# Decay attention with a gated expert layer: scores in four rounds of two banks, the first decay rows without TensorE, and a new order

## The chip, the cores and the metric

The kernel runs on one core of one Trainium2 chip. The metric is the device time of one execution in microseconds. Engines are named as the profile names them: PE (TensorE matmul), PEld (its weight loads), DVE (VectorE), ACT (ScalarE), POOL (GpSimd), SP (SyncE, which here only issues transfers).

## What is computed

For 8 batches of 8 heads (sequence 576, head dimension 64) the reference does this, and then an expert layer on the 128 tokens of each batch that score highest:

```python
scores = scale * q @ k.T                       # 576 x 576 for each head
cum    = cumsum(log(clip(f, 1e-4, 1)))         # 576 numbers for each head
scores = where(causal, -1e9, scores + cum[i] - cum[j])
attn   = softmax(scores); x = attn @ v         # all heads side by side: 576 x 512
s      = x @ w_gate; idx = top 128 of s
out[idx] = x[idx] + sigmoid(s[idx]) * (relu(x[idx] @ w1) @ w2)
```

The term `cum[i]` is the same for a whole row and falls out of the softmax, so the kernel only needs `-8 * cum[j]`, one row of 576 numbers for each head, spread over all 128 partitions. It calls that tile `e`.

## The kernel before, in words

The work goes in 32 pairs of heads. For a pair, `q` and `k` lie in SBUF with one head on partitions 0 to 63 and the other on 64 to 127 (tiles `rq` and `rk`). The scores of the two heads are computed together, head by head in the two halves of the array, into two PSUM banks, one for each head. There are eight banks in all. The lower triangle of a head is cut into row blocks `i` of 128 queries (`i` = 0, 1, 2, 3, and `NF` = 4 for the last 64) and these into six units, listed in `units` (L542): block 3 with keys 0 to 384, block 3 with keys 384 to 576, block 1, block 2, the 64 by 64 corner, and block 0. Each unit takes two fresh banks (two `ps` tokens).

What follows a unit:

- L631, DVE: one instruction for each head adds the decay, takes the row's extreme and writes the sum to SBUF (`p`). Its decay comes from `e`, or from `m`, which POOL makes out of `e` by masking it along the diagonal (L412). When the last such instruction on a bank is done, the bank is free.
- L684, ACT: exp over the row block, with the row sum.
- L703, PE: transposes of the exps into a pair of banks; L350 (ACT, POOL) or L354 (DVE) copies them to SBUF (`pt`).
- L786, PE: the product with `v`; copies (`ot`); L844, PE: transposes back; L849, DVE: division by the row sums.
- L859 and L863: the gate's scores; after four pairs a batch is complete and its expert layer follows (L1006 ranks, L1059 gathers, L1122 to L1183 are the matmuls, L1194 scatters).

The decay: `f` for all 64 heads is loaded with one head on each partition (L370), clipped (L373), its logarithm is taken (L380, ACT), then a running sum (L384, DVE), then times -8 (L389). The result is stored to DRAM (`eq`, L407), and for heads 2 to 63 a transfer spreads a row of `eq` over 128 partitions (L513, `e<-eq`). For heads 0 and 1 PE spreads it: `bcast` (L462) multiplies a selecting column of the identity with the rows (L470) into two banks for each head, and copies bring them to `es[0]` and `es[1]`.

The order of all this is not written out by hand. Each piece is entered with `add` (L64): its cost by engine, what it comes after, which tokens (banks, buffers) it takes and gives back, and a number `place`. `Flow.run` (L122) then lays out the schedule when the kernel is built: for each engine it looks at the pieces that could start within `EPS` of the earliest one and takes the one with the smallest `place`. An engine's instructions run in the order that comes out of this. A piece that may run on several engines goes to the one where it would end first, after `BD` microseconds have been added for DVE. Before `HALF` microseconds PE's costs count double. Some 35 constants (L212 to L256) enter the places.

Of the kernel before, what the change touches and what calls it, by code (L numbers as in the profile page):

```python
# [17 lines left out]
P = 128  # L18
# [12 lines left out]
class Flow:  # L31
# [146 lines left out]
def kernel(  # L178
# [30 lines left out]
    NRT = (cap + P - 1) // P  # L209
    FR = 3 * R  # L210

    BD = 0.595  # L212
    WP = 17
    WQ = 0
    R0 = -28.266
    X0 = -83.254
    XE_ = -237.817
    XH_ = 1.479
    XM_ = 144.372
    XB_ = -3.268  # L220
    XN_ = -284.728
    XO_ = -358.772
    XU_ = 1.204
    XQ_ = 299.353
    XR_ = 137.373
    XG_ = -107.42
    PL4 = -284.738
    GW = 587.406
    EPS = 0.121
    LOOK = 13  # L230
    PR = -110.796
    PL = 37.918
    PS = 148.049
    PV = 3.402
    PM = -218.946
    PE_ = 78.604
    PC = 15.176
    PB = -122.458
    PD = 13.682
    VO = 29.244  # L240
    VD = 1
    GD = 0.1
    WS = -43.026
    WD = 316.377
    WL = 239.211
    RK = 41.91
    RD = 9.792
    XP = 21.468
    GO = 4.807
    GS = 2.051  # L250
    GL = 29.298
    LG = 2.69
    SB = 3
    SX = 2.5
    SP = -3.444
    TU = 0.061  # L256

    const = ctx.enter_context(tc.tile_pool(name="const", bufs=1))
# [9 lines left out]
    def bank(tk):  # L268
        return banks[:, tk.at * 512:(tk.at + 1) * 512]
# [92 lines left out]
    def load(fn, kb, n=1, slow=0.0, **kw):  # L362
        return add({"sp": 0.63 * n}, fn, lat=1.6 + slow, dma=kb / 240, **kw)
# [3 lines left out]

    def t_fs(e):
        z["fs"] = moe.tile([BH, S], F32, tag="h", name="fs")
        nc.sync.dma_start(out=z["fs"], in_=f)  # L370

    def t_clamp(e):
        nc.vector.tensor_scalar(z["fs"], z["fs"], 1e-4, 1.0, ALU.max, ALU.min)  # L373

    def t_ones(e):
        z["ones"] = work.tile([BH, S], F32, tag="ot", name="ones", bufs=2)
        nc.vector.memset(z["ones"], 1.0)

    def t_ln(e):
# [1 line left out]

    def t_scan(e):
        z["cum"] = moe.tile([BH, S], F32, tag="srow", name="cum")
        nc.vector.tensor_tensor_scan(out=z["cum"], data0=z["ones"], data1=z["fs"], initial=0.0,  # L384
                                     op0=ALU.mult, op1=ALU.add)
# [5 lines left out]
    tk_h, tk_ot, tk_srow = Token("h"), Token("ot"), Token("srow")  # L391
    tk_ep = Token("hth", 3)
    d_fs = load(t_fs, 144, place=-60, take=[tk_h])
    d_ones = add({"dve": 0.6}, t_ones, place=-60, take=[tk_ot])
    d = add({"dve": 0.47}, t_clamp, after=[d_fs], place=-59)
    d = add({"act": 0.68}, t_ln, after=[d], place=-58, give=[tk_h])

    def t_warm(e):

        warm = small.tile([P, 1], F32, tag="none", name="warm", bufs=2)  # L400
        nc.scalar.activation(warm[0:BH], z["ones"][:, 0:1], AF.Exp)

    add({"act": 1.5}, t_warm, after=[d, d_ones], place=-57.5)
    d_scan = add({"dve": 1.35}, t_scan, after=[d, d_ones], place=-57, take=[tk_srow], give=[tk_ot])
    d_ep = add({"dve": 0.45}, t_ec, after=[d_scan], place=-56, take=[tk_ep], give=[tk_srow])
# [51 lines left out]

    d_zero = add({"dve": 0.4}, t_zero, place=-70)

    spread = {}  # L460

    def bcast(h):  # L462

        tk = [Token("ps") for _ in range(2)]
        st = {}

        def eb(e):
            st["b"] = [bank(t) for t in tk]
            for g in range(2):
                nc.tensor.matmul(st["b"][g][:, 0:S // 2], ident[0:BH, h:h + 1].broadcast_to([BH, P]),  # L470
                                 z["ec"][:, g * (S // 2):(g + 1) * (S // 2)], start=True, stop=True)

        def ec(e, g):
            copy_on(e, es[h][:, g * (S // 2):(g + 1) * (S // 2)], st["b"][g][:, 0:S // 2])

        x = spread[h] = add({"pe": 1.0}, eb, after=[d_ep, d_ident], place=-20 + h, take=tk, give=[tk_ep], kind="av")
        return [add({**act(S // 2), **dve(S // 2)}, lambda e, g=g: ec(e, g), after=[x], place=-50 + h, give=[tk[g]])
                for g in range(2)]

    raws, ops, tks = {}, {}, {}  # L480
    dec = {}
    decused = {}
# [1 line left out]
    def pair_ops(p):  # L484
        pl = 9 * p - PL
        r = p % 2
        tk = tks[p] = {"q": Token("rq", 6), "k": Token("raw", 6)}

        def t_k(e):
            t = raws["k", p] = rawp.tile([P, S], F32, tag="raw", name=f"rk{p}")  # L490
# [61 lines left out]
    def pair_parts(p):  # L552
# [19 lines left out]
        copied = []  # L572
        sums = []
        exps, late, scored, ready, tk_nm = {}, {}, {}, {}, {}
        for u, (i, k0, k1) in enumerate(units):
            n = k1 - k0
            t = p * NT + (AT[u] - LOOK) // 2
            ahead = [moved[min(t, len(moved) - 1)]] if t >= 0 and moved else []
            if p == 0 and u > 1:
                ahead = ahead + list(spread.values())  # L580
            place = p * NU + AT[u] * XU_ - LOOK * NU / 8
            tk_n, tk_b = [], [Token("ps"), Token("ps")]
            if i == 2 or i == 3 and k0 == 0:
                late[i] = Token(f"p{i % 2}", i)
                tk_n.append(late[i])
            if i == NF:
                late[NF] = Token("p4")
                tk_n.append(late[NF])

            def s0(e, u=u, i=i, k0=k0, tk_b=tk_b):  # L590
                st["sc", u] = [bank(t) for t in tk_b]
                if i == 2 or i == 3 and k0 == 0:
                    st["pw", i] = pw.tile([P, PAT[i] + 2 * WB[i]], F32, tag=f"p{i % 2}", name=f"p{p}_{u}", bufs=2)

            def sc(e, u=u, i=i, k0=k0, k1=k1):
                for hh in range(2):
                    rows = slice(hh * D, hh * D + D)
                    nc.tensor.matmul(st["sc", u][hh][:, 0:k1 - k0], q_rows(raws["q", p], hh, i), raws["k", p][rows, k0:k1],  # L598
                                     start=True, stop=True)

            def part(hh, i):

# [14 lines left out]

                return t if hh == 0 or i == NF else t.rearrange("p (b c) -> p b c", c=R)

            def m(e, hh, x0, x1, in1, key, first, u=u, i=i, k0=k0, into=into, blocks=blocks):  # L620
# [15 lines left out]
            if i < 2 or i == 3 and k0:  # L636
                ahead = ahead + [scored[i + 2 if i < 2 else i]]
            x2 = add(row(n), lambda e, s0=s0, sc=sc: (s0(e), sc(e)), after=ops[p] + ahead, place=place,
                     take=tk_b + tk_n, give=list(tks[p].values()), kind="row")
            scored[i] = x2  # L640
            for hh in range(2):
                h = 2 * p + hh
                def e_(n_, h=h):
# [628 lines left out]
```

## Time and profile before

| | |
|---|---|
| median of 3 runs | 419.74 us (418.47 to 420.68) |
| the profiled execution | 424.2 us, span 422.4 us |
| busy: PE / DVE / ACT / POOL | 392.2 / 324.0 / 324.3 / 210.9 us |
| weight loads on PE (PEld) | 268.8 us |

The span runs from the first to the last instruction of the execution; 1.8 us of the execution's time lie outside it. The end of a matmul is modelled, so the busy time of PE tells less than the waits of its weight loads.

### The profile page before, as it was taken

The page shows a single profiled execution, that of the slowest core. Times are in us where ns is not written, and L with a number is a line of the kernel's source. Part 1 is how long each engine was busy: PE and PEld are TensorE (multiplying, and loading weights), DVE is VectorE, ACT ScalarE, POOL GpSimd, SP SyncE. Part 2 cuts the span into 40 slices and gives each one's busy share as a digit, 9 for nine tenths or more (in the row PEclk, how much of TensorE's full clock was granted, in tenths as well). Part 3 has the DMA queues.
Part 4 walks back from the last instruction along what each step waited for, and adds up shares of the span by engine and source line. Part 5 has one row for each costly group of instructions (what it writes and reads, how often), then busy time and mean ns, then how long its engine had stood idle before and what let it go on. Part 6 is the DMA issues. An engine that isn't in the chain of part 4 may idle for free. (4 is left out here: it accounts for less than half of the span.)

```text
span 422.4 us, 12058 instructions
## 1 busy us (share of the span) xinstructions
PE 392.2 (93%) x3873; PEld 268.8 (64%) x3873; DVE 324.0 (77%) x1356; ACT 324.3 (77%) x1008; POOL 210.9 (50%) x368
## 2 busy tenths in 40 slices
PE   4689999899999899899999999999999999999995
PEld 3266765566656675566576676757666675768773
DVE  3577668787998699889968977789776987688721
ACT  4699999999999787999697888879797887712220
POOL 5486786977686642655156355423646323223100
PEclk9889999999999999999999999999999999999998
DMA  6688778888687636775375636655565403202100
GB/s 199 187 223 236 193 215 234 240 225 242 195 238 201 196 113 189 212 194 165 113 203 172 190 104 177 198 171 137 172 167 189 119 30 111 90 25 82 50 25 26
DMA packets 76870, 68.10 MB, mean 161 GB/s; under 512 B 47715, under 2 KB 56966, under 8 KB 76806
## 3 DMA queue, kind: packets, MB, share of 16 engines
q1 hardware_dynamic: 75446, 62.98, 52.5%
q0 software_dynamic: 1280, 4.20, 2.9%
q8 instruction: 31, 0.51, 0.5%
q14 instruction: 33, 0.27, 0.2%
q10 hardware_dynamic: 80, 0.15, 0.1%
HBM read 55.59 MB, written 11.70 MB: 159 GB/s over the span
## 5 line engine op out<-in xcount | busy, mean ns | idle before, releaser
L684 ACT ACTIVATE p<-p,nm 128x576 f32<-128x576 f32 (+4 forms) x288 | 165.4, 581 | 13.1 <-DVE nm L631 12.9
L412 POOL TENSOR_SCALAR_AFFINE_SELECT m<-e 128x384 f32<-128x384 f32 (+3 forms) x256 | 108.3, 449 | 112.7 <-DMA e<-eq 73.8
L598 PE MATMUL banks<-rk,rq 64*128 64x192 f32 (+4 forms) x768 | 127.5, 429 | 13.0 <-DMA rq<-in_qk_dram 5.3
L350 ACT COPY pt<-banks 128x512 f32<-128x512 f32 (+4 forms) x311 | 113.0, 428 | 16.7 <-PE banks L703 12.1
L631 DVE CUSTOM_DVE_ANT_0 p<-banks,m 64x64 f32<-64x64 f32 (+3 forms) x256 | 99.8, 419 | 14.5 <-PE banks L598 6.9
L598 PEld LDWEIGHTS banks<-rk,rq 64*128 64x128 f32 x768 | 71.8, 190 | 45.7 <-DVE nm L631 16.0
L786 PE MATMUL banks<-pt,v 128*64 128x448 f32 (+4 forms) x768 | 92.3, 392 | 0.6 <-DVE nm L631 0.5
L786 PEld LDWEIGHTS banks<-pt,v 128*64 128x64 f32 x768 | 47.2, 137 | 44.7 <-issue 27.1
L703 PE MATMUL banks<-ident,p 64*128 64x64 f32 x1472 | 68.4, 229 | 6.7 <-DVE nm L631 4.1
L703 PEld LDWEIGHTS banks<-ident,p 64*128 64x128 f32 x1472 | 59.7, 140 | 19.6 <-DVE nm L631 8.6
L859 POOL TENSOR_TENSOR gj<-x,wg 128x640 f32<-128x640 f32 x32 | 49.4, 1545 | 43.5 <-DVE x L849 26.5
L684 ACT ACTIVATION_READ_ACCUMULATOR p<-p,nm 128x1 f32 x288 | 55.8, 194 | 0.0
L631 DVE CUSTOM_DVE_ANT_0 p<-banks,e 128x384 f32<-128x384 f32 x64 | 35.2, 552 | 13.2 <-ACT e L350 4.0
L1006 DVE TENSOR_SCALAR_CACHE_REDUCE j<-srow,sg 128x384 uint8<-128x384 f32 (+6 forms) x72 | 41.2, 572 | 2.0
L849 DVE TENSOR_TENSOR x<-banks,rn 128x640 f32<-128x640 f32 x32 | 26.3, 822 | 17.7 <-PE banks L844 11.1
L350 ACT COPY ot<-banks 128x128 f32<-128x128 f32 (+1 forms) x58 | 20.3, 394 | 14.5 <-PE banks L786 14.4
L631 DVE DVE_READ_ACCUMULATOR2_ANT nm<- 128x1 f32 (+1 forms) x384 | 31.2, 81 | 0.0
L631 DVE CUSTOM_DVE_ANT_0 p<-banks,m,nm 128x192 f32<-128x192 f32 x64 | 26.6, 416 | 5.5 <-DVE nm L631 1.0
L863 DVE TENSOR_REDUCE gu<-gj 128x5 f32<-128x640 f32 x32 | 25.8, 805 | 5.0 <-POOL gj L859 4.6
L1194 POOL DMA_INDIRECT out_dram<-xe,idx x8 | 8.2, 1022 | 38.3 <-DVE xe L1190 34.9
L1122 PE MATMUL banks<-w1h,xth 128*128 128x512 f32 x64 | 26.0, 406 | 0.9 <-ACT xth L1084 0.7
L1175 PE MATMUL banks<-w2h,hth 128*128 128x512 f32 x64 | 26.2, 409 | 0.0
(91 smaller groups left out, 416.1 us busy)
## 6 DMA issues: line engine op xcount, KB each, us to landing
e<-eq SPq DMA_DIRECT2D x62, 288.0 KB
rk<-in_qk_dram SPq DMA_DIRECT2D x32, 288.0 KB
out_dram<-x SPq DMA_DIRECT2D x16, 512.0 KB
rq<-in_qk_dram SPq DMA_DIRECT2D x32, 144.0 KB
rq<-in_qk_dram SPq DMA_DIRECT2D x32, 128.0 KB
v<-in_v_dram SPq DMA_DIRECT2D x32, 128.0 KB
v<-in_v_dram SPq DMA_DIRECT2D x32, 80.0 KB
srow<-sd SPq DMA_DIRECT2D x7, 320.0 KB
```

Source lines behind the costliest of these rows:

```text
L350: nc.scalar.copy(d, s_)
L412: nc.gpsimd.affine_select(out=dst, in_=src, pattern=w, compare_op=ALU.is_ge, fill=NEG, base=base, channel_multiplier=1)
L598: nc.tensor.matmul(st["sc", u][hh][:, 0:k1 - k0], q_rows(raws["q", p], hh, i), raws["k", p][rows, k0:k1], start=True, stop=True)
L631: nc.vector.tensor_tensor_reduce(out=into(hh, i, r_, x0, x1), in0=blocks(b_[r_, x0 - k0:x1 - k0], hh, i), in1=blocks(in1(), hh, i), scale= ...
L684: nc.scalar.activation(x, x, AF.Exp, bias=st["nm", hh, i], scale=-1.0, accum_out=l)
L703: nc.tensor.transpose(tp[:, g, col:col + R], src, ident[g * R:g * R + R, g * R:g * R + R])
L786: nc.tensor.matmul(avb[p, g][par * D:(par + 1) * D, qo + q0 - g * SPL:qo + q1 - g * SPL], vt[:, j, par * D:(par + 1) * D], pt[:, off:off + ...
L849: nc.vector.tensor_tensor(out=xhs[key][:, :, w_ * P:(w_ + 1) * P].rearrange("p c (h d) -> p c h d", h=2), in0=st["tb"][:, :, 0:NCH * D].re ...
L859: nc.gpsimd.tensor_tensor(out=gj, in0=xhs[key][:, :, w0:w1], in1=wg[:, hb * HB + w0:hb * HB + w1].unsqueeze(1).broadcast_to([P, NCH, P]), ...
L1006: nc.vector.tensor_scalar(junk[0:n, 0:w, :], src, sg()[0:n, c:c + 1], None, op, ALU.add, accum_out=cnt[0:n, k, c:c + 1])
L1122: nc.tensor.matmul(q["hp", n][0:nr, :], q["xth"][:, c, 0:nr], r_[:, c, cs], start=(c == 0 and k_ == 0), stop=False)
L1175: nc.tensor.matmul(q["yp"][0:nr, :], q["hth"][:, c, 0:nr], r_[:, c, :], start=(c == 0 and k_ == 0), stop=False)
```

## The change

1. The six units become four groups. Two groups consist of two units each, which share a round's two banks side by side: block 3's keys 384 to 576 (192 columns) with block 1 (320 columns), and block 0 (192) with the corner (64).
2. For heads 0 and 1 the row of `f` is spread over 128 partitions by a transfer, and clip, logarithm, running sum and factor are computed on all partitions (DVE, ACT, DVE, ACT), straight into `es[0]` and `es[1]`. `bcast` and its matmuls, banks and copies go. The computation for all 64 heads stays, since `eq` feeds the others; its load of `f` is issued by ACT's queue.
3. `HALF`, `EPS`, `BD` and nearly all constants of the places get other values, so that the order of every engine is laid out anew.

```diff
-    HALF = 22.0
+    HALF = 12.0
...
-    BD = 0.595
+    BD = 14.28
...
-    EPS = 0.121
+    EPS = 0.003
...
     def t_fs(e):
         z["fs"] = moe.tile([BH, S], F32, tag="h", name="fs")
-        nc.sync.dma_start(out=z["fs"], in_=f)
+        nc.scalar.dma_start(out=z["fs"], in_=f)
...
+    def first(h):
+        e_, m_ = es[h], ms[h][:, 0:S]
+        def f_clamp(e):
+            (nc.vector if e == "dve" else nc.gpsimd).tensor_scalar(e_, e_, 1e-4, 1.0, ALU.max, ALU.min)
+        def f_ln(e):
+            nc.scalar.activation(e_, e_, AF.Ln)
+        def f_scan(e):
+            nc.vector.tensor_tensor_scan(out=m_, data0=z["ones"], data1=e_, initial=0.0, op0=ALU.mult, op1=ALU.add)
+        def f_ec(e):
+            nc.scalar.mul(e_, m_, -8.0)
+        x = load(lambda e: nc.sync.dma_start(out=e_, in_=f[h:h + 1, :].broadcast_to([P, S])), 288, place=-62 + h)
+        x = add({"dve": 0.6}, f_clamp, after=[x], place=-59.5 + h)
+        x = d_lf[h] = add({"act": 0.53}, f_ln, after=[x], place=-59 + h)
+        x = add({"dve": 1.35}, f_scan, after=[x, d_ones], place=-58.5 + h, give=[tk_ot])
+        return add({"act": 0.53}, f_ec, after=[x], place=-58 + h)
+    d_first = [first(h) for h in range(2)]
...
-    add({"act": 1.5}, t_warm, after=[d, d_ones], place=-57.5)
+    add({"act": 1.5}, t_warm, after=[d, d_ones] + list(d_lf.values()), place=-58.6)
...
-    def bcast(h):
...
-                le = bcast(h)
+                le = [d_first[hh]]
...
-    units = [(3, 0, 384), (3, 384, S), (1, 0, 320), (2, 0, 448), (NF, 0, R), (0, 0, FR)]
-    AT = (0, 1, 2, 4, 5, 6)
+    groups = [[(3, 0, 384)], [(3, 384, S), (1, 0, 320)], [(2, 0, 448)], [(0, 0, FR), (NF, 0, R)]]
+    AT = (0, 1, 4, 5)
...
+            tk_n, tk_b = [], [Token("ps", len(group)), Token("ps", len(group))]
...
+            def sc(e, u=u, group=group, tk_b=tk_b):
+                st["sc", u] = [bank(t) for t in tk_b]
+                o = 0
+                for i, k0, k1 in group:
...
+                    for hh in range(2):
+                        rows = slice(hh * D, hh * D + D)
+                        nc.tensor.matmul(st["sc", u][hh][:, o:o + k1 - k0], q_rows(raws["q", p], hh, i), raws["k", p][rows, k0:k1],
+                                         start=True, stop=True)
+                    o += k1 - k0
```

## Rows read from the trace of the kernel before

**Rows 1.** The page's busy times: us, share of the span, instructions

```profile
span 422.4 us, 12058 instructions
PE 392.2 (93%) x3873; PEld 268.8 (64%) x3873; DVE 324.0 (77%) x1356; ACT 324.3 (77%) x1008; POOL 210.9 (50%) x368
```

**Rows 2.** Windows: stretch, its us, then busy us (instructions) PE, PEld, DVE, ACT, POOL

```profile
25.00:50.00 25.00, 24.54 (x280) 17.15 (x280) 18.94 (x87) 24.45 (x80) 19.43 (x31) 0.96 0.77 214
50.00:75.00 25.00, 24.18 (x288) 15.83 (x286) 18.45 (x77) 23.85 (x80) 16.59 (x27) 1.00 0.79 224
75.00:100.00 25.00, 23.48 (x305) 15.81 (x303) 18.93 (x82) 23.62 (x79) 19.58 (x33) 1.00 0.83 225
...
200.00:250.00 50.00, 49.12 (x498) 33.70 (x499) 42.83 (x193) 40.34 (x124) 19.69 (x34) 1.00 0.52 149
```

**Rows 3.** Timeline of the start: start us, us, engine, line; idle before it, releaser

```profile
0.74 0.60 SPq L370 DMA_DIRECT2D fs<-in_f_dram  x1
3.62 0.45 DVE L373 TENSOR_SCALAR fs<-fs 64x576 f32<-64x576 f32 x1 [1.79 <-DMA fs<-in_f_dram]
4.11 0.68 ACT L380 ACTIVATE fs<-fs 64x576 f32<-64x576 f32 x1 [2.09 <-DVE fs L373]
4.81 1.28 ACT L401 ACT_TABLE_LOAD   x1
4.82 1.35 DVE L384 TENSOR_TENSOR_SCAN cum<-ones,fs 64x576 f32<-64x576 f32 x1 [0.75 <-ACT fs L380]
...
6.21 0.62 DVE L389 TENSOR_SCALAR ec<-cum 64x576 f32<-64x576 f32 x1
...
9.95 0.56 DVE L631 CUSTOM_DVE_ANT_0 p<-banks,e 128x384 f32<-128x384 f32 x1 [3.13 <-ACT e L350]
...
12.10 0.61 SPq L513 DMA_DIRECT2D e<-eq  x1
...
12.34 0.56 DVE L631 CUSTOM_DVE_ANT_0 p<-banks,e 128x384 f32<-128x384 f32 x1 [0.85 <-ACT e L350]
...
20.80 0.56 DVE L631 CUSTOM_DVE_ANT_0 p<-banks,e 128x384 f32<-128x384 f32 x1 [3.04 <-DMA e<-eq]
```

**Rows 4.** Waits of PE's weight loads, 25 to 350 us: total us, times, longest

```profile
PEld banks L598 <- DVE nm L631: 11.0, 27, 0.8
PEld banks L598 <- ACT pt L350: 10.2, 28, 0.8
```

**Rows 5.** The same waits, 140 to 350 us

```profile
PEld banks L598 <- ACT pt L350: 6.4, 17, 0.8
PEld banks L598 <- DVE nm L631: 4.7, 14, 0.6
PEld banks L598 <- DVE x L849: 3.3, 6, 1.0
```

**Rows 6.** DVE's copies (L354) by stretch: us, busy us (count)

```profile
25.00:50.00 25.00, 1.31 (x2) 0.96 0.77 214
50.00:75.00 25.00, 1.36 (x3) 1.00 0.79 224
75.00:100.00 25.00, 1.57 (x3) 1.00 0.83 225
```

**Rows 7.** ACT's lines 25 to 125 us, the copy that most resembles them: busy, mean ns

```profile
L350 ACT COPY pt<-banks 128x512 f32<-128x512 f32 x20 | 10.9, 589 | 0.6 <-DVE pt L354 0.6
```

**Rows 8.** Lines of DVE in the first 25 us: a reduction of 192 columns and its read-out

```profile
L631 DVE CUSTOM_DVE_ANT_0 p<-banks,m,nm 128x192 f32<-128x192 f32 x4 | 1.7, 416 | 0.4 <-PE banks L470 0.2 <-DVE nm L631 0.2
L631 DVE DVE_READ_ACCUMULATOR2_ANT nm<- 128x1 f32 x18 | 1.5, 81 | 0.0
```

**Rows 9.** Timeline at 209 us: turns in one pair of banks, and the copies of its halves

```profile
209.13 0.66 PE L703 MATMUL banks<-ident,p 64*128 64x64 f32 x16
...
209.84 1.07 ACT L350 COPY pt<-banks 128x512 f32<-128x512 f32 x2 [0.39 <-PE banks L703]
```

**Rows 10.** PE's lines over the whole span: the matmuls of the 320-column unit

```profile
L598 PE MATMUL banks<-rk,rq 64*128 64x320 f32 x128 | 29.7, 483 | 3.5 <-DVE x L849 1.4 <-ACT pt L350 1.3 <-DVE nm L631 0.3
```

More of the change, by code (lines that the diff above doesn't have):

```diff
@@ L210 @@
     FR = 3 * R
-    BD = 0.595
+    BD = 14.28
     WP = 17
     WQ = 0
[L215 to L228, printed above, removed]
-    EPS = 0.121
-    LOOK = 13
[L231 to L240, printed above, removed]
+    R0 = -77.756
+    X0 = -68.439
+    XE_ = -327.929
+    XH_ = 7.854
+    XM_ = 53.367
+    XB_ = -7.168
+    XN_ = -63.025
+    XO_ = -208.515
+    XU_ = 1.335
+    XQ_ = 493.393
+    XR_ = 125.313
+    XG_ = 21.837
+    PL4 = -478.193
+    GW = 98.553
+    EPS = 0.003
+    LOOK = 13
+    PR = -210.485
+    PL = -23.333
+    PS = 534.017
+    PV = 76.813
+    PM = -72.798
+    PE_ = 32.812
+    PC = -113.684
+    PB = -32.5
+    PD = -24.608
+    VO = 5.153
     VD = 1
     GD = 0.1
[L243 to L251, printed above, removed]
+    WS = -47.45
+    WD = 405.121
+    WL = 461.576
+    RK = 62.425
+    RD = 6.657
+    XP = 4.552
+    GO = 25.288
+    GS = 0.584
+    GL = 84.612
     LG = 2.69
@@ L254 @@
     SX = 2.5
-    SP = -3.444
+    SP = -185.065
     TU = 0.061
@@ L389, in t_ec @@
         nc.vector.tensor_scalar(z["ec"], z["cum"], -8.0, None, ALU.mult)
[L391 to L393 removed]
+    tk_h, tk_ot, tk_srow = Token("h"), Token("ot", 3), Token("srow")
+    tk_ep = Token("hth")
+    def first(h):
[13 more added lines that the diff above has]
+        return add({"act": 0.53}, f_ec, after=[x], place=-58 + h)
@@ L394 @@
+    d_lf = {}
+    d_fs = add({"act": 0.62}, t_fs, place=-63, take=[tk_h], lat=2.2)
     d_ones = add({"dve": 0.6}, t_ones, place=-60, take=[tk_ot])
-    d = add({"dve": 0.47}, t_clamp, after=[d_fs], place=-59)
-    d = add({"act": 0.68}, t_ln, after=[d], place=-58, give=[tk_h])
+    d_first = [first(h) for h in range(2)]
+    d = add({"dve": 0.47}, t_clamp, after=[d_fs], place=-60.6)
+    d = add({"act": 0.68}, t_ln, after=[d], place=-60.5, give=[tk_h])
     def t_warm(e):
         warm = small.tile([P, 1], F32, tag="none", name="warm", bufs=2)
-        nc.scalar.activation(warm[0:BH], z["ones"][:, 0:1], AF.Exp)
@@ L403 @@
-    add({"act": 1.5}, t_warm, after=[d, d_ones], place=-57.5)
-    d_scan = add({"dve": 1.35}, t_scan, after=[d, d_ones], place=-57, take=[tk_srow], give=[tk_ot])
-    d_ep = add({"dve": 0.45}, t_ec, after=[d_scan], place=-56, take=[tk_ep], give=[tk_srow])
+        nc.scalar.activation(warm[0:BH], z["ones"][0:BH, 0:1], AF.Exp)
+    add({"act": 1.5}, t_warm, after=[d, d_ones] + list(d_lf.values()), place=-58.6)
+    d_scan = add({"dve": 1.35}, t_scan, after=[d, d_ones], place=-58.2, take=[tk_srow], give=[tk_ot])
@@ L407 @@
+    d_ep = add({"dve": 0.45}, t_ec, after=[d_scan], place=-58.1, take=[tk_ep], give=[tk_srow])
     st_eq = add({"act": 0.62}, lambda e: nc.scalar.dma_start(out=eq[:, :], in_=z["ec"]), lat=2.5, after=[d_ep], place=PR,
@@ L458 @@
     d_zero = add({"dve": 0.4}, t_zero, place=-70)
-    spread = {}
-    def bcast(h):
[L464 to L478, printed above, removed]
     raws, ops, tks = {}, {}, {}
@@ L574, in pair_parts @@
         exps, late, scored, ready, tk_nm = {}, {}, {}, {}, {}
-        for u, (i, k0, k1) in enumerate(units):
-            n = k1 - k0
+        plan = []
+        for u, group in enumerate(groups):
             t = p * NT + (AT[u] - LOOK) // 2
             ahead = [moved[min(t, len(moved) - 1)]] if t >= 0 and moved else []
-            if p == 0 and u > 1:
-                ahead = ahead + list(spread.values())
             place = p * NU + AT[u] * XU_ - LOOK * NU / 8
[L582 to L590, printed above, removed]
-                st["sc", u] = [bank(t) for t in tk_b]
[L592 to L599, printed above, removed]
@@ new lines, in pair_parts @@
+            tk_n, tk_b = [], [Token("ps", len(group)), Token("ps", len(group))]
+            for i, k0, _ in group:
+                if i == 2 or i == 3 and k0 == 0:
+                    late[i] = Token(f"p{i % 2}", i)
+                    tk_n.append(late[i])
+                elif i == NF:
+                    late[NF] = Token("p4")
+                    tk_n.append(late[NF])
+                elif i < 2 or i == 3:
+                    ahead = ahead + [scored[i + 2 if i < 2 else i]]
+            def sc(e, u=u, group=group, tk_b=tk_b):
+                st["sc", u] = [bank(t) for t in tk_b]
+                o = 0
+                for i, k0, k1 in group:
+                    if i == 2 or i == 3 and k0 == 0:
+                        st["pw", i] = pw.tile([P, PAT[i] + 2 * WB[i]], F32, tag=f"p{i % 2}", name=f"p{p}_{u}", bufs=2)
+                    for hh in range(2):
[3 more added lines that the diff above has]
+                    o += k1 - k0
@@ L601, in part @@
+            x2 = add({"pe": sum(row(k1 - k0)["pe"] for _, k0, k1 in group)}, sc, after=ops[p] + ahead, place=place,
+                     take=tk_b + tk_n, give=list(tks[p].values()), kind="row")
+            o = 0
+            for i, k0, k1 in group:
+                scored.setdefault(i, x2)
+                plan.append((u, i, k0, k1, o, x2, tk_b, place))
+                o += k1 - k0
+        for u, i, k0, k1, co, x2, tk_b, place in plan:
             def part(hh, i):
@@ L618, in blocks, with m @@
                 return t if hh == 0 or i == NF else t.rearrange("p (b c) -> p b c", c=R)
-            def m(e, hh, x0, x1, in1, key, first, u=u, i=i, k0=k0, into=into, blocks=blocks):
+            def m(e, hh, x0, x1, in1, key, first, u=u, i=i, k0=k0 - co, into=into, blocks=blocks):
                 b_ = st["sc", u][hh]
@@ L634, in m @@
                 st["nm", hh, i] = nm if i < NF else t[:, g:g + 1]
[L636 to L640, printed above, removed]
             for hh in range(2):
```

6 lines of the change are left out of this document (3 added, 3 removed).

## Prediction

> **What bounds the kernel now.** I read the page's busy times first [rows 1]. PE is busy 93% of the span, but its weight loads only 64%; so PE is seldom without a matmul in flight, and yet its queue often stands at a load. The windows by stage [rows 2] come next, since the share of the span is a mean. Two stages differ. From 25 to 100 us ACT is busy 24.45 + 23.85 + 23.62 = 71.92 of 75 us, 96%, while DVE stays at 75%: ACT sets the pace, and only 3.1 us of it are free. In the stretch at 200 to 250 us ACT has fallen to 40.34 of 50 and DVE to 42.83, and PE shows 49.12: the expert layers now run between the pairs, and what PE waits for decides. The waits of the weight loads say what that is: a new round of scores needs two free banks and finds them still held by a DVE reduction (L631), an ACT copy (L350) or DVE's division (L849) [rows 4, 5]. The start [rows 3] is a stage of its own: DVE's first reduction begins at 9.95, after 3.13 us in which it waited for the decay of head 0, then it waits 0.85 us for head 1 and, in pair 1, 3.04 us for a transfer from `eq`. After the attention only expert layers are left; the change touches nothing there but their places.
>
> The Trainium skill (Perfetto Trace Analysis, Identifying the Most-Contended Engine) says that matmul busy time is a bad measure of PE's distance from its limit and names the weight loads' busy share instead. By that, 93% would leave nothing to gain and 64% does leave something; the waits below show the same without it.
>
> **The change, part by part.**
>
> *The start.* Before, the chain to `e` of head 0 is load, clip 0.45, logarithm 0.68, sum 1.35, factor 0.62, then PE and copies, to 9.95 [rows 3]. After, PE and the copies fall out, but DVE computes three times instead of once: 3 x 0.45 + 3 x 1.35 + 0.62 = 6.0 us where 2.4 stood (the durations on 64 partitions are taken for 128, as both have 576 columns). Its input lands no sooner than 3.62, so all three are through at 9.6 at the earliest. ACT has three logarithms (2.04), then the table load 1.28 that the exp needs, then the factor, for which I take the logarithm's 0.68: from 4.11, one clip after landing, that is 4.11 + 2.04 + 1.28 + 0.68 = 8.1, and some 0.6 more if the spread load, twice as large as the 144 KB one, lands later. So `e` of head 0 can be there at 8.1 to 8.7 and that of head 1 some 0.7 us later, where the second reduction on an `e` began at 12.34. But the three scans stand ahead of the reductions on DVE unless the third is put behind, and then `eq` is late. Bounds: 1.3 us before 9.95 and the 0.85 us gap may go, and the 3.04 us wait in pair 1 if its load is issued sooner; what is gained ahead of that wait is lost in it unless it goes too, so the gain is at most 3.0 us. At the other end `ec` ends at 9.6 instead of 6.8, 2.8 us later; the first `e<-eq` was issued at 12.10, and with a store that lands as long after its issue as the load of `f` did (2.9 us), it can't go before 12.6 to 13.1: 1.0 us lost. I take 1.0 gained, the middle. The two spread loads put 1.2 us (two issues of 0.60) ahead of `rk` and `rq` on SP's queue; PE's scores then come that much later and still stand ready before DVE is. That cover is gone only if the reductions begin before about 8 us. The load of `f` moves from SP to ACT's queue, ahead of the table load there, and costs 0.6 us that the transfer's landing hides.
>
> *Four rounds for six.* Matmuls, reductions and exps are the same in number and size, so no engine's work shrinks. What can go is the wait for banks: 192 rounds become 128. In 25 to 350 us the loads of L598 waited 11.0 + 10.2 = 21.2 us for reductions and copies [rows 4]; a third of it is 7.1 us, the upper bound. In the first stage ACT sets the pace and a PE that waits less waits elsewhere, so I count from 140 us on: 6.4 + 4.7 + 3.3 = 14.4 [rows 5], a third is 4.8 us. The lower bound is nothing, since each remaining round holds its banks over two reductions. I take 4.8: a second unit in the same banks asks for no free bank at all.
>
> *Copies.* With `BD` at 14.28 a copy goes to DVE only where ACT is that far behind, which is never; `BD` was 0.595. In 25 to 100 us DVE made 2 + 3 + 3 = 8 copies [rows 6]. On ACT the nearest row is 0.589 us each [rows 7]: 4.7 us more on an engine with 3.1 us free. Later ACT has room. The ends are 0 (the copies fall where ACT would wait for a transpose) and 4.7; I take 2.4, the middle, as no row shows the exchange.
>
> *Places.* The new constants reorder everything. They add no instruction, and no row prices them; their bounds are those of the rivals.
>
> Sum: 424.2 (the profiled execution, span 422.4 and 1.8 around it) - 1.0 - 4.8 + 2.4 = 420.8. The median of the runs is 4.5 below the profiled execution, so 416.3, 0.8% less than 419.74. What this kernel's measurement can tell from no change is about 0.5%, 2.1 us: faster means under 417.6, slower over 421.8.
>
> **The rivals.**
>
> *All of it is collected.* The start gives 3.0, the rounds 7.1, the copies fall into waits: -10.1, so 409.6. For it: the waits are spread over 55 places of at most 0.8 us [rows 4], such as an order laid out anew can cover. Against it: ACT at 96% in the first stage.
>
> *ACT keeps the pace.* The rounds give nothing, since what PE saves it waits at the next transpose for ACT; -1.0 + 2.4 = +1.4, so 421.1. For it rows 2, first stage; against it the fall of ACT to 81% later.
>
> *The reader waits for the whole bank.* In a shared round DVE's reduction of the first 192 columns may have to wait until PE has written the second part. At 209 us [rows 9] both halves of a pair of banks were copied only after the last of 16 turns (209.13 + 0.66, copy at 209.84), though the first half was written by half of them. The second part's matmul is 0.483 us [rows 10], in 32 rounds; if as many of them are exposed as rounds waited before (55 of 192, 0.29), that is 32 x 0.29 x 0.483 = 4.5 us. It eats the rounds' gain: -1.0 - 4.8 + 2.4 + 4.5 = +1.1, so 420.8.
> The Trainium skill (PSUM — Partial Sum Buffer, PSUM bank collisions raise a hardware error) asks for guards by bank and quadrant, not by address, which would make every such reduction wait so; the copies in rows 9 agree with it.
>
> *Held banks: slower.* Place: the 64 two-part rounds. Each bank is held for one more reduction, 0.416 + 0.081 = 0.50 us [rows 8], and the round behind it, which needs two, comes later by that wherever it waited already: 64 x 0.29 = 18.6 rounds, 9.3 us. -1.0 - 4.8 + 2.4 + 9.3 = +5.9, so 425.6. For it: L631 is the first among those waited for [rows 4]. Against it: a round that is written later also takes its banks for fewer separate turns. It decides from 0.29 us for each of these rounds on: 18.6 x 0.29 = 5.3, which undoes the 3.4 us gained and adds the 2.1 that can be told.
>
> **How the numbers follow.** Forecast 0.40 (its own range 413 to 419); all collected 0.20; ACT keeps the pace 0.13; whole bank 0.10; held banks 0.17. Faster: 0.32 of the forecast's 0.40 and 0.20, together 0.52, with 0.01 from the others. Same: 0.08 of the forecast, 0.16 of the two cases near 421. Slower: 0.17 and the rest of those two, 0.23. The range reaches from 407, a little under the case with all collected (the places have no price), to 425, near the held banks' 425.6; outside are about 0.08 below and 0.10 above.
>
> **What would show it.** No L470; the first reduction on an `e` near 9 us, with three scans ahead of it, and the next no longer behind a gap; ACT 96% or more busy from 25 to 100 us and no L354 copies; waits of L598's loads for L631, L350 and L849 from 140 us on down from 14.4 to about 10 us; the last product with `v` some 3 us sooner. Wrong it would be if L598's waits stay or grow (held banks), if L631 waits more for L598 (whole bank), if the first 100 us get longer (copies), or if the time comes from the last expert layers, for which I count nothing.

## The result, and the profile after

The changed kernel takes 425.43 us (median of 4 runs, 424.19 to 426.11) against 420.21 us for the kernel before beside it (4 runs): ratio 1.0128, 95% interval [1.0088, 1.0168]. On two other chips it came to 1.0070 [1.0038, 1.0101] and 1.0082 [1.0041, 1.0123]. It is about 0.9% slower, some 4 us; 0.8% faster was forecast, and 425.43 lies just outside the range. Executions that took over 1.5% more than the fastest of their kernel are left out of the ratios (of the twelve of k2 below six, of h1's three), and the ratios are not quite the quotients of the medians. The two profiled executions are not a measure of the change: that of before stood 4.5 us above its median, that of the changed kernel (425.63 us, span 423.9) on it.

The page's busy times, in the columns of [rows 1]:

```profile
span 423.9 us, 11994 instructions
PE 387.1 (91%) x3865; PEld 276.8 (65%) x3865; DVE 311.3 (73%) x1343; ACT 328.6 (78%) x1024; POOL 211.4 (50%) x369
```

DVE has 12.7 us less and PE 5.1 us less to do than before, ACT 4.3 us more, and the span is longer. So PE and DVE, with less to do, wait more. The windows, in the columns of [rows 2] (the value behind the engines is the granted clock):

```profile
25.00:50.00 25.00, 22.57 (x248) 15.44 (x248) 16.12 (x75) 23.93 (x77) 13.77 (x22) 0.93 0.79 232
50.00:75.00 25.00, 22.33 (x262) 14.71 (x262) 18.65 (x89) 24.89 (x83) 21.98 (x32) 1.00 0.81 230
75.00:100.00 25.00, 22.55 (x255) 15.49 (x251) 16.43 (x74) 22.15 (x74) 16.43 (x30) 0.93 0.76 212
```

ACT is busy 23.93 + 24.89 + 22.15 = 70.97 of 75 us from 25 to 100, about what it was (71.92). In the same stretch PE issued 248 + 262 + 255 = 765 matmuls where [rows 2] have 873. The start, in the columns of [rows 3]:

```profile
0.73 0.56 ACTq L370 DMA_DIRECT2D fs<-in_f_dram  x1
...
0.74 0.88 SPq L410 DMA_DIRECT2D e<-in_f_dram  x2
...
5.90 0.45 DVE L373 TENSOR_SCALAR fs<-fs 64x576 f32<-64x576 f32 x1 [4.06 <-DMA fs<-in_f_dram]
...
7.10 1.35 DVE L384 TENSOR_TENSOR_SCAN cum<-ones,fs 64x576 f32<-64x576 f32 x1 [0.38 <-ACT fs L380]
8.37 1.33 DVE L405 TENSOR_TENSOR_SCAN m<-ones,e 128x576 f32<-128x576 f32 x1
...
8.74 4.65 PE L604 MATMUL banks<-rk,rq 64*128 64x384 f32 x16 [8.74 <-DMA rq<-in_qk_dram]
...
11.02 1.60 DVE L405 TENSOR_TENSOR_SCAN m<-ones,e 128x576 f32<-128x576 f32 x1 [0.60 <-ACT e L402]
...
12.54 0.53 DVE L648 CUSTOM_DVE_ANT_0 p<-banks,e 128x384 f32<-128x384 f32 x1
...
14.28 1.58 SPq L518 DMA_DIRECT2D e<-eq  x3
```

The three sums stand ahead of the first reduction (L648 is the old L631), which starts at 12.54 where [rows 3] have 9.95. Of these 2.6 us, 2.3 come from the first clip (5.90 for 3.62): it waited 4.06 us for `f`. From the clip on, the chain takes 12.54 - 5.90 = 6.64 us, before 9.95 - 3.62 = 6.33: three sums on DVE cost what the detour over PE and the copies cost. The issue of `e<-eq` moved from 12.10 to 14.28. The views of the two loads say how long they took:

```profile
L370 ACTq DMA_DIRECT2D fs<-in_f_dram x1: 565/565/565, 0.7 to 0.7; - x1
...
DMA to landing us min/median/max: 5.1/5.1/5.1
...
L410 SPq DMA_DIRECT2D e<-in_f_dram x2: 402/412/421, 0.7 to 1.2; - x2
...
DMA to landing us min/median/max: 5.4/5.4/5.4
```

The load of `f` landed 2.9 us after its issue (0.74 to 3.62) when it was the first on SP's queue and the next load was issued 0.65 us later. It takes 5.1 us from ACT's queue, beside the two spread loads of 288 KB. The waits of the weight loads ahead of score rounds (L604 is the old L598), 140 to 350 us, in the columns of [rows 5]:

```profile
PEld banks L604 <- DVE nm L648: 3.2, 9, 0.7
PEld banks L604 <- ACT pt L350: 1.8, 5, 0.5
PEld banks L604 <- DVE x L861: 1.3, 2, 1.0
```

These are 6.3 us where [rows 5] sum to 14.4: 8.1 us gone, more than the 4.8 of the forecast. What came in their place is on DVE. First the kernel before, then the changed one: DVE's reductions by form, 25 to 380 us; the columns are busy time, mean ns of one, and the idle time before them with its releasers.

```profile
L631 DVE CUSTOM_DVE_ANT_0 p<-banks,m 128x448 f32<-128x448 f32 x60 | 35.9, 617 | 1.6 <-PE banks L598 0.9 <-PE banks L703 0.5 <-ACT p L684 0.3
L631 DVE CUSTOM_DVE_ANT_0 p<-banks,e 128x384 f32<-128x384 f32 x60 | 32.9, 551 | 5.8 <-PE banks L598 3.5 <-DMA rq<-in_qk_dram 1.6 <-issue 0.4
...
L631 DVE CUSTOM_DVE_ANT_0 p<-banks,m,nm 128x192 f32<-128x192 f32 x60 | 24.9, 416 | 5.1 <-PE banks L598 1.0 <-DVE nm L631 0.9 <-ACT pt L350 0.3
...
DVE p L631 <- PE banks L598: 11.2, 27, 1.7
```

```profile
L648 DVE CUSTOM_DVE_ANT_0 p<-banks,m 128x448 f32<-128x448 f32 x61 | 37.6, 618 | 13.5 <-PE banks L604 13.2 <-issue 0.3
L648 DVE CUSTOM_DVE_ANT_0 p<-banks,e 128x384 f32<-128x384 f32 x60 | 32.5, 553 | 14.7 <-PE banks L604 10.9 <-ACT pt L350 3.0 <-ACT s L350 0.3
...
L648 DVE CUSTOM_DVE_ANT_0 p<-banks,m,nm 128x192 f32<-128x192 f32 x60 | 24.8, 414 | 6.8 <-PE banks L604 3.1 <-POOL m L437 1.6 <-POOL gj L871 1.2
...
DVE p L648 <- PE banks L604: 30.3, 24, 5.2
```

The last line of each is from the list of DVE's waits in the same stretch: total us, times, longest. DVE waited 11.2 us for scores and now waits 30.3, in fewer and longer waits. PE waits less for banks, and DVE waits more for PE. Whether it is the rounds, the start or the order that does this, this profile can't tell, since all three changed at once.

### The profile page after: what moved, and what is told of

Read it like the earlier page. It is cut to its first block, busy times and chain, and to the rows that moved or that the text cites. A ratio compares the mean times of both kernels' runs of the same rounds, so it can differ in the third digit from the quotient of the medians.

```text
span 423.9 us, 11994 instructions
## 1 busy us (share of the span) xinstructions
PE 387.1 (91%) x3865; PEld 276.8 (65%) x3865; DVE 311.3 (73%) x1343; ACT 328.6 (78%) x1024; POOL 211.4 (50%) x369
## 5 line engine op out<-in xcount | busy, mean ns | idle before, releaser
L696 ACT ACTIVATE p<-p,nm 128x320 f32<-128x320 f32 (+4 forms) x288 | 166.8, 586 | 6.7 <-DVE nm L648 6.1
L604 PE MATMUL banks<-rk,rq 64*128 64x192 f32 (+4 forms) x768 | 123.2, 433 | 16.4 <-DMA rq<-in_qk_dram 8.7
L350 ACT COPY pt<-banks 128x256 f32<-128x256 f32 (+4 forms) x320 | 120.3, 430 | 14.5 <-PE banks L715 12.9
L648 DVE CUSTOM_DVE_ANT_0 p<-banks,m 128x320 f32<-128x320 f32 (+3 forms) x256 | 99.0, 418 | 20.9 <-PE banks L604 17.3
L604 PEld LDWEIGHTS banks<-rk,rq 64*128 64x128 f32 x768 | 79.1, 198 | 37.1 <-DVE nm L648 13.3
L715 PEld LDWEIGHTS banks<-ident,p 64*128 64x128 f32 x1472 | 63.2, 143 | 22.6 <-issue 6.9
L715 PE MATMUL banks<-ident,p 64*128 64x64 f32 x1472 | 71.5, 231 | 7.0 <-ACT pt L350 2.6
L798 PEld LDWEIGHTS banks<-pt,v 128*64 128x64 f32 x768 | 45.9, 137 | 47.8 <-issue 30.7
L648 DVE CUSTOM_DVE_ANT_0 p<-banks,e 128x384 f32<-128x384 f32 x64 | 34.7, 553 | 16.4 <-PE banks L604 12.7
L350 ACT COPY ot<-banks 128x128 f32<-128x128 f32 x64 | 23.1, 402 | 21.1 <-PE banks L798 21.0
L861 DVE TENSOR_TENSOR x<-banks,rn 128x640 f32<-128x640 f32 x32 | 26.2, 822 | 13.6 <-PE banks L856 11.5
L648 DVE CUSTOM_DVE_ANT_0 p<-banks,m,nm 128x192 f32<-128x192 f32 x64 | 26.5, 414 | 8.6 <-PE banks L604 4.3
L648 DVE DVE_READ_ACCUMULATOR2_ANT nm<- 128x1 f32 (+1 forms) x384 | 31.0, 81 | 0.0
L1147 ACT ACTIVATE h<-banks 128x512 f32<-128x512 f32 x16 | 9.6, 602 | 20.9 <-PE banks L1141 20.9
```

Source lines behind the costliest of these rows:

```text
L604: nc.tensor.matmul(st["sc", u][hh][:, o:o + k1 - k0], q_rows(raws["q", p], hh, i), raws["k", p][rows, k0:k1], start=True, stop=True)
L648: nc.vector.tensor_tensor_reduce(out=into(hh, i, r_, x0, x1), in0=blocks(b_[r_, x0 - k0:x1 - k0], hh, i), in1=blocks(in1(), hh, i), scale= ...
L696: nc.scalar.activation(x, x, AF.Exp, bias=st["nm", hh, i], scale=-1.0, accum_out=l)
L715: nc.tensor.transpose(tp[:, g, col:col + R], src, ident[g * R:g * R + R, g * R:g * R + R])
L798: nc.tensor.matmul(avb[p, g][par * D:(par + 1) * D, qo + q0 - g * SPL:qo + q1 - g * SPL], vt[:, j, par * D:(par + 1) * D], pt[:, off:off + ...
L861: nc.vector.tensor_tensor(out=xhs[key][:, :, w_ * P:(w_ + 1) * P].rearrange("p c (h d) -> p c h d", h=2), in0=st["tb"][:, :, 0:NCH * D].re ...
```

## The experiments

Theory S (start): the loss comes from the landing of `f` and all that hangs on it. Theory O (order): it comes from the order laid out anew. Rival R (rounds): the shared banks cost more than they bring. Rival D: DVE's sums standing in a row cost the time, not the landing. The expectations call the order theory P (for places) in the first runs (f1 to f6), and the landing theory L in h1 and h2. Ratios are to the kernel before on the same chip, with 95% intervals.

### One part alone, the order laid out anew each time

Four kernels keep two of the three parts or one, and the planner lays out a new order for each:

```diff
 f1:  after, with
-    groups = [[(3, 0, 384)], [(3, 384, S), (1, 0, 320)], [(2, 0, 448)], [(0, 0, FR), (NF, 0, R)]]
+    groups = [[(3, 0, 384)], [(3, 384, S)], [(1, 0, 320)], [(2, 0, 448)], [(NF, 0, R)], [(0, 0, FR)]]
 f2:  after, with
-                le = [d_first[hh]]
+                le = bcast(h)                     # and the load of f on SP's queue again
 f3:  after, with the constants of before
 f4:  before, with first(h) in place of bcast(h); its constants stay
```

> The changed kernel with six rounds of scores again; new start and new places stay. Theory P (the new places cost the time): still slow, 424 to 427 us, and DVE still waits some 30 us for score matmuls, since the order by places and not the rounds makes the scores late. Theory R (rounds shared by two units hold banks longer and make the reader wait for the whole bank): the 5.2 us come back, 419 to 422 us, and the reductions of 192 columns wait for PE as little as before (1.0 us in all, 4.3 after the change). Theory S (the start costs it): 424 to 426 us, the first reduction still at 12.5 us.

> The changed kernel with the decay of heads 0 and 1 spread by PE again; four rounds and new places stay. Theory S: the first reduction comes back from 12.5 to about 10 us and the time falls by about that, 2.5 us, to some 423 us. Theories P and R: what the start loses is given back in the first 150 us, where ACT sets the pace; 425 us, within 1 us of the changed kernel.

> The changed kernel's four rounds and new start, with all constants of the places (and HALF, EPS, BD) as before. Theory P: back to 419 to 422 us or under it, and DVE's wait for score matmuls back towards 11 us. Theory R: 424 us or more, since the shared rounds are still there. Theory S: 422 to 423 us.

> The kernel before with nothing changed but the start (heads 0 and 1 computed on all partitions, three loads of f). Theory S: 2 to 3 us slower than before, 422 to 423 us, with the first reduction near 12.5 us. Theories P and R: no difference from before that can be told, 419 to 421 us.

Measured: six rounds (f1) 1.0256 [1.0226, 1.0287]; old start (f2) 1.0110 [1.0070, 1.0150]; old constants (f3) 1.0206 [1.0160, 1.0252]; only the start (f4) 1.0190 [1.0143, 1.0237]. Then the other two single parts, and the kernel before once more, for a second trace:

```diff
 f5:  before, with the four rounds; its constants stay, and
-            if p == 0 and u > 1:
+            if p == 0 and u > 0:
 f6:  before, with the constants of after
```

> The kernel before with nothing changed but the rounds: four of two banks instead of six. Since the planner found no way with its old condition, the second round of pair 0, too, comes after the spreading of heads 0 and 1 by PE. Theory R: slower than before, 424 us or more, the reductions of 192 columns waiting for PE. Theory P: no slower than before, 416 to 421 us, and fewer waits of weight loads for banks.

> The kernel before, six rounds and old start, with the new constants alone. Theory P: 424 us or more, DVE waiting 20 to 30 us for score matmuls. Theory R or S: 419 to 422 us.

> The kernel before once more with a profile, as a second trace beside the first, whose own time of 424.2 us lies 4 us above the median. If that trace is usual: 422 us of span again and the same waits. If it is not: a span of 417 to 419 us, and the difference shows in which stage the first trace lost time that other executions do not lose.

Measured: only the rounds (f5) 1.0105 [1.0084, 1.0125]; only the constants (f6) 1.0254 [1.0229, 1.0278]; before again (f7) 422.28 us beside a median of 422.54. Every cell is slower than the kernel before; four of the six are slower than all parts together (1.0128 at most), and f2 and f5 are about as slow. Read as prices the three single parts would add to 5.5%, where all three at once cost 1%. So these cells don't price the parts: each has an order of its own that no one fitted to it. How much that can be, the smallest edit shows.

### The same pieces in a slightly other order

```diff
-    EPS = 0.121
+    EPS = 0.15
```

> The kernel before with EPS 0.15 instead of 0.121 and nothing else: the same pieces, the same start and rounds, only laid out in another order from the early pairs on. Theory O (an order is fitted to its constants, and any other costs): 1.010 to 1.025, as in the runs in which one part was changed under constants fitted to another. If an order laid out anew costs nothing by itself: 0.996 to 1.004.

Measured: 1.0416 [1.0373, 1.0460]. No piece's work is changed, only which ready piece is taken first and, for a few copies, the engine (ACT has 1011 instructions for 1008). The windows of one stretch, first before, then this kernel:

```profile
100.00:150.00 50.00, 46.20 (x462) 30.89 (x459) 43.20 (x183) 45.55 (x148) 33.78 (x54) 1.00 0.72 208
```

```profile
100.00:150.00 50.00, 41.95 (x490) 27.91 (x492) 41.51 (x190) 42.53 (x138) 34.42 (x56) 0.95 0.79 221
```

PE, ACT and DVE are all busy less there, by 4.25, 3.02 and 1.69 us, and the granted clock is 0.95 for 1.00. An order alone can cost 4%, four times the result that is to be explained. From here on the order is therefore held.

### One part alone, the order kept

The order of every engine was recorded piece by piece, and the planner's choice was replaced by the recorded rank:

```diff
-            best = {}
-            for t in self.ready:
...
+            for t in self.ready:
+                rank, e = ORDER[t["key"]]
+                s = self.start(t, e)
+                if s is not None and (pick is None or rank < pick[0][1]):
+                    pick = ((s, rank, t["n"]), e, t)
```

A merged round stands where the earlier of its two units stood; the pieces of the new start stand at the head of their engines. The choice of DVE or ACT for a copy is part of the recorded order.

> The order of the kernel before kept piece by piece; only the start is the new one, its pieces put where the changed kernel has them. Theory S (the start in itself costs, as the loads of f land 5 us after their issue instead of 2.9): the first reduction at 12.4 us instead of 9.95, and of these 2.5 us most arrives at the end, 1.5 to 3 us slower. Theory O (what costs is that an order fitted to one kernel is laid out anew for another): with the order kept, 0 to 1 us slower, although the new start under the old constants, with a new order, was 7.6 us slower.

> The order of the kernel before kept; only the rounds are shared, block 1's scores at once behind block 3's second part, block 0's together with the corner's. Theory R (shared rounds cost, by banks held and by the reader's wait for the whole bank): 2 to 9 us slower. Theory O: -5 to +1 us, the fewer rounds gaining up to the 4.8 us that the waits before them allow, although under the old constants with a new order they were 4.2 us slower.

> The order of the changed kernel kept piece by piece; only the start is the old one. Theory S: 1.5 to 3 us faster than the changed kernel, so 1.006 of the kernel before. Theory O: within 1 us of the changed kernel, 1.010 to 1.015, since in it the rest of the order, not the start, is what costs.

> The order of the changed kernel kept; only the rounds are six again, the two units of a shared one behind each other in banks of their own. Theory R: faster than the changed kernel, 1.000 to 1.008. Theory O: slower than it or the same, 1.013 to 1.025, since six rounds ask for more banks than this order has free at that time.

Measured: before's order with the new start (g1) 1.0056 [1.0024, 1.0089]; before's order with four rounds (g2) 0.9946 [0.9914, 0.9978]; the changed order with the old start (g3) 0.9974 [0.9935, 1.0013]; the changed order with six rounds (g4) 1.0910 [1.0852, 1.0969]. The last is no price of the rounds: an order made for four rounds serves six badly, presumably since each needs two free banks of its own. In before's order, g1 and g2 are prices: the start is a loss and the rounds are a gain. Theory S has one part right, and R falls there. g3 lies below what either theory expected of it (1.006, or 1.010 and more); it comes again below, as k2. In g1 the first reduction starts at 12.24, in g3 at 9.48.

Why do the rounds bring 0.54%, 2.3 us, and not 4.8? In g2 (its lines are some 200 higher: L806 is the old L598, L851 the old L631) the waits of PE's weight loads from 140 to 350 us are

```profile
PEld banks L806 <- DVE nm L851: 6.2, 10, 1.2
PEld banks L806 <- ACT pt L555: 3.0, 9, 0.8
...
PEld banks L806 <- DVE x L1064: 1.8, 4, 1.0
```

together 11.0 us, 3.4 less than [rows 5]. DVE's reductions of 25 to 380 us in g2, by form as above, and the line from DVE's waits:

```profile
L851 DVE CUSTOM_DVE_ANT_0 p<-banks,m 128x448 f32<-128x448 f32 x60 | 35.9, 618 | 0.2
L851 DVE CUSTOM_DVE_ANT_0 p<-banks,e 128x384 f32<-128x384 f32 x60 | 33.0, 552 | 7.8 <-PE banks L806 4.7 <-DMA rq<-in_qk_dram 2.3 <-DMA e<-eq 0.7
...
L851 DVE CUSTOM_DVE_ANT_0 p<-banks,m,nm 128x192 f32<-128x192 f32 x60 | 25.0, 416 | 11.5 <-PE banks L806 8.1 <-DVE nm L851 1.4 <-ACT p L899 1.0
...
DVE p L851 <- PE banks L806: 19.5, 32, 1.8
```

The reductions of block 3's last 192 columns, which open a shared round, wait 8.1 us for PE where they waited 1.0; the forms of 320 columns and more hardly change. (In the other shared round, of the corner and block 0, the wait changes hands: 6.8 us and under 0.6, before 0.6 and 5.2.) One place in g2's timeline shows what they wait for; the twelve matmuls are four each of 384, 192 and 320 columns, in this order:

```profile
215.63 1.79 PE L806 MATMUL banks<-rk,rq 64*128 64x384 f32 x12
...
217.39 0.42 DVE L851 CUSTOM_DVE_ANT_0 p<-banks,m,nm 128x192 f32<-128x192 f32 x1 [0.30 <-PE banks L806]
```

The matmuls of the 192 columns had ended by 216.9, and DVE had been free since 217.09; the reduction begins when the 320 columns beside them end, at 217.4. That is the prediction's rival of the whole bank, in the very form it named: the reader of the first part waits while PE writes the second. That these waits are what the rounds' gain lacks is argued from their size, not tested.

### The landing or the sums

Two kernels keep the changed order and edit only the start. In h1 the load of `f` for all heads goes first on SP's queue and the two spread loads behind it; in h2 head 1's sum moves behind the first three reductions as well:

```diff
 h1 and h2:
-        nc.scalar.dma_start(out=z["fs"], in_=f)
+        nc.sync.dma_start(out=z["fs"], in_=f)     # ahead of the two spread loads
 h2 too:  m_ <- scan (head 1) behind the third reduction, e_ <- m_ behind the first exp
```

> The changed kernel once more, beside the kernel before on the same chip as the three below, so that they can be set against it. Both theories: 1.009 to 1.017 of the kernel before.

> The changed kernel's order kept; only the load of f for all heads goes first on SP's queue, and the two spread loads stand behind it, instead of all three starting at 0.73 us. Theory L (the new start is late because its three loads share the transfer engines and land 5.1 to 5.4 us after their issue): f lands at 3.5 us again, the sum over all heads ends 2 us sooner, the spread loads land at 5.5 to 6.5, and the first reduction moves from 12.5 to 10 to 11 us; 1.5 to 2 us faster than the changed kernel. Theory D (it is late because DVE has three sums to make before the first reduction): the first reduction moves by less than 0.5 us and so does the end.

> As h1, and DVE makes the sum of head 1 only behind the first three reductions of head 0 (ACT's factor for head 1 behind the first exp). Theory D: this is what helps, the first reduction at 9 to 9.5 us instead of 12.5, and the time falls to that of the changed order with the old start, 0.996 to 1.002. Theory L: 0.5 to 1 us beyond h1, as head 1 comes later by what head 0 gains.

Measured on one chip: the changed kernel (h0) 1.0070 [1.0038, 1.0101]; `f` first (h1) 0.9994 [0.9961, 1.0028]; the sum behind too (h2) 1.0130 [1.0081, 1.0179]. The timeline of h1's start (L581 is L373, L607 is L399, L812 is L604, L857 is L648):

```profile
0.74 0.59 SPq L578 DMA_DIRECT2D fs<-in_f_dram  x1
...
1.39 1.04 SPq L618 DMA_DIRECT2D e<-in_f_dram  x2
...
3.57 0.45 DVE L581 TENSOR_SCALAR fs<-fs 64x576 f32<-64x576 f32 x1 [1.74 <-DMA fs<-in_f_dram]
...
5.40 0.46 DVE L607 TENSOR_SCALAR e<-e 128x576 f32<-128x576 f32 x1 [1.37 <-DMA e<-in_f_dram]
...
11.20 0.53 DVE L857 CUSTOM_DVE_ANT_0 p<-banks,e 128x384 f32<-128x384 f32 x1
```

`f` lands at 3.57 again, as before the change, and the first reduction comes 1.21 us sooner than in h0 (12.41). Rival D expected less than 0.5. One transfer's place and queue (the two weren't changed apart) give back 0.76% on the same chip, 3.2 us (the medians over all executions are 423.23 and 419.43), all that the change had lost there.

How 1.21 us become 3.2 this start doesn't show. Head 1's first reduction comes only 0.38 us sooner (13.50 for 13.88), and the first `e<-eq` is issued 0.97 later (15.07 for 14.10). h1 and h0 have the same order on every engine, so their traces can be laid side by side, piece by piece: h1 leads by 0.46 us from 25 to 75 us, by 1.4 at 100, 3.3 at 150 and 4.0 at the end. Most of the lead grows between 75 and 150 us, where the granted clock of h0 is below full in three stretches of 25 us (0.93, 0.97, 0.97) and h1's is not. From 25 to 200 us, first h0, then h1:

```profile
25.00:100.00 75.00, 66.87 (x785) 45.33 (x785) 51.78 (x233) 71.95 (x237) 51.81 (x82) 0.98 0.78 226
100.00:200.00 100.00, 93.86 (x1042) 64.74 (x1042) 86.19 (x391) 91.61 (x297) 61.79 (x100) 0.98 0.68 195
```

```profile
25.00:100.00 75.00, 66.44 (x804) 44.39 (x800) 51.89 (x234) 72.64 (x240) 54.00 (x84) 1.00 0.81 231
100.00:200.00 100.00, 94.92 (x1051) 64.17 (x1053) 88.34 (x401) 92.81 (x304) 62.62 (x106) 1.00 0.70 201
```

Over twelve executions each, the mean granted clock was 0.977 in h0 and 0.987 in h1. So about half a microsecond of the gain comes straight from the start; the rest goes with the clock and with waits in the middle of the kernel, and how the start leads to these was not tested.

In h2 the first reduction is still sooner, 10.95, but head 1 is late instead:

```profile
12.97 0.48 DVE L857 CUSTOM_DVE_ANT_0 p<-banks,m 128x320 f32<-128x320 f32 x1
...
13.38 1.35 DVE L613 TENSOR_TENSOR_SCAN m<-ones,e 128x576 f32<-128x576 f32 x1
15.49 0.56 DVE L857 CUSTOM_DVE_ANT_0 p<-banks,e 128x384 f32<-128x384 f32 x1 [0.75 <-ACT e L616]
```

The second head's reduction starts at 15.49 where the changed kernel had 14.01. Taking a sum out of the row made it worse, so D's remedy is none. What the row of sums costs by itself h2 doesn't price: head 1 comes later by it, and at 157 us PE waits 3.62 us for a gather, where h1 has no such wait.

### The square of two orders and two starts

The cell that was missing, both parts in before's order (k1), with the changed kernel (k0) and the changed order with the old start (k2) on one chip:

> The changed kernel, beside the two below on one chip: 1.005 to 1.015 of the kernel before, as in its two runs so far.

> Both parts, the new start and the four rounds, in the order of the kernel before. If the two parts add, as they measured alone (0.56% lost by the start, 0.54% gained by the rounds), 1.000, between 0.997 and 1.004. If the new order is what costs the changed kernel its 1%, this is below it by 0.7% or more; if the start alone costs it, because the later start isn't made good by anything, this is near the changed kernel, 1.006 to 1.012.

> The changed kernel's order and rounds with the old start, beside the two above. If the start costs the same in either order, this is 0.5% below the changed kernel; if the start costs more in the new order, 1% or more below it, and near 0.997 again.

Measured: k0 1.0082 [1.0041, 1.0123]; k1 1.0051 [1.0022, 1.0080]; k2 1.0040 [1.0002, 1.0077]. With the runs above:

| | old start | new start |
|---|---|---|
| before's order, six rounds | 1 | 1.0056 |
| before's order, four rounds | 0.9946 | 1.0051 |
| changed order, four rounds | 0.9974, 1.0040 | 1.0128, 1.0070, 1.0082 |
| changed order, four rounds, `f` first | | 0.9994 |

The start costs 0.56% (g1) and 1.05% (k1 less g2, two chips) in before's order. In the changed order k0 less k2 is 0.42% on one chip, and that is not told from nothing: the intervals overlap, and the medians over all executions are 423.51 and 423.86 us. The rounds bring 0.54% with the old start; with the new the difference is 0.05%, between two chips. The order, with the copies that go with it, costs 0.31% (k0 less k1) with the new start and 0.28% or 0.94% with the old; the two of one chip have intervals that overlap, so this term is not told from nothing by itself. Whether the two parts add can't be told either: their sum is 1.0002 and k1 lies 0.49% above it, about the uncertainty of that difference (0.5%, from the three intervals). Neither theory takes the whole loss; S has the larger share.

## Why the prediction was wrong, point by point

*The start: the step that failed.* The prediction had the input landing "no sooner than 3.62", and "some 0.6 more" for the spread load, and took 1.0 us gained, with 1.0 lost as its bound. But the landing of `f` was carried over from a row in which that load was issued ahead of all others. Beside two loads of 288 KB, and from ACT's queue, it took 5.1 us, so that the clip, the sums, the first reduction and the first `e<-eq` came 2.2 to 2.6 us later, the store of `eq` 3.6 later (10.45 for 6.85), and `rk` and `rq` too: PE's first score matmul began at 8.74 for 5.31. The chain behind the landing was nearly right, 6.0 us for DVE's part where 6.64 passed, but it held no gain: the path over PE had taken 6.33. Even with `f` at 3.57 (h1) the first reduction starts at 11.20, 1.25 after before's, since head 0's own load lands only at 5.40. The price is 0.56% to 1.05%, 2.3 to 4.4 us on 419.4, against -1.0: an error of 3.3 to 5.4 us, the largest. In g1 some 1.3 us of it are there at 25 us already (traces side by side). The Trainium skill (DMA: Bandwidth & Descriptors, Latency and other measured facts) says that HBM's access latency rises with load, from 0.2 to 2 us; the trace agrees in direction, with 2.9 and 5.1 us for one load, though it doesn't show which part of the way the 2.2 us are spent on.

*The rounds: right in sign, too large.* Waits for banks fell as forecast and more. Of the 4.8 us, 2.3 came back with the old start; with the new it was 0.2 (0.05% of 419.4), which is not told from nothing or from 2.3. What may have eaten the rest is in g2's rows: 7.1 us of new waits of the 192-column reductions for the second part of a shared round. The rival of the whole bank had put 4.5 us on it, with a chance of 0.10. It deserved more: its sign, named ahead, is there (L631 waits more for L598). Part of those waits is off the path, or nothing would have been gained. Having the reductions of a shared round wait for their own part alone was not tried.

*Held banks.* Its 425.6 is the time that came out, by chance. Its sign would have been that waits of L598's loads stay or grow; they fell from 14.4 to 6.3, and to 11.0 with the order kept. The slower bank turnover isn't in the traces.

*Copies.* No copy is left on DVE, as foreseen, and ACT's busy time from 25 to 100 us fell by 0.95 us instead of growing by up to 4.7; over the whole span it grew by 4.3. The 2.4 us can't be told from the order's own price, with which they were measured: 0.28% to 0.94%, 1.2 to 3.9 us together.

*Places.* "No row prices them" was right, and leaving the term at nothing was not: an order can cost 4% (EPS) at unchanged work. In the changed kernel it shows as fewer but longer waits of DVE for scores, before the 448 and 384 column reductions (13.2 and 10.9 us where 0.9 and 3.5 stood), and these are there with the old start too (k2 13.0 and 11.5). Since k2 and g3 stand at 1.0040 and 0.9974, most of that waiting can't be on the path. One wait of the new order holds up ACT and DVE too: PE stands before the transposes of the rows gathered for an expert layer (L1089) until the gather lands,

```profile
PE banks L1089 <- DMA xe<-out_dram,idx: 2.3, 2, 2.0
```

2.0 us at 152 us, 2.2 in k0, 0.7 in h0. In the kernel before, g2, k1 and h1 no matmul waits for a gather. Behind it the granted clock is 0.93 from 150 to 200 us in the changed kernel and in k0, where PE is busy 46.3 and 46.1 us; it is 1.00 in h0, h1 and before (47.4, 48.7 and 47.5). This is no term of the prediction. What it costs by itself wasn't tested.

*The sum by measured terms*, along the square: rounds -0.54%, start +1.05%, order and copies +0.31%, together +0.82%, 3.4 us. These are differences between neighbouring cells, so they add up to k0 whatever the causes; the other two measurements of the change have 1.28 and 0.70%. Open are how the order's part splits into places, copies and clock, and why the chips differ by half a per cent.

*A version that is faster than both:* before's start and order with the four rounds (g2), 0.9946 of the kernel before, 420.85 us on a chip where that one takes 423.43.

## What to carry to other kernels

Price a part of a change with the order of everything else held: a planner that lays out a new order for each variant can add 1 to 4% that has nothing to do with the part. A load's landing time belongs to what is in flight beside it (or to its queue; the two were not told apart here); when loads are added at the start, put the one on which most work hangs first in the queue. And a wait that vanishes on one engine should be looked for on the engine that fed from it before it is booked as time won.

## What the runs showed of the hardware that was not expected

- One load of 144 KB at the start of the kernel took 2.9 us to land when nothing else was issued for 0.65 us, and 4.8 to 5.4 us (g1 and k0; k1) beside two of 288 KB that were issued in the same microsecond on another queue; issued 0.65 us ahead of them on their queue, it landed after 2.8 us again (0.74 to 3.57).
- The granted clock of one and the same kernel differs between executions: the changed kernel's profiled ones had means of 0.970, 0.986 and 0.983, at spans of 423.9, 418.1 and 421.7 us. The profile above has 0.93 in two of its early windows where before had 0.96 and 1.00. With `f` first the profiled execution has 0.994 and a span of 414.1. The spread of the executions goes with it: of h0's twelve the three with the highest mean clock (0.983 to 0.987) took 419.84 to 422.83 us, the three with the lowest (0.970 and 0.971) 424.87 to 425.87. And the kernels differ in it: on one chip its mean over the executions is 0.990 in the kernel before, 0.987 in h1 and 0.977 in the changed kernel. How much of the loss the clock makes was not measured by itself.
